# A fused linear-attention and gated-MLP block on one Trainium2 core: output weights from sixteen 32-column products, wider GELU pieces, and new engine orders

## The chip, the cores and the metric

The kernel runs on one core of one Trainium2 chip. The metric is the device time of one execution in microseconds (us); the number quoted for a kernel is the median of its runs.

The engines are named as in the profile: PE is TensorE's matmul stream, PEld its weight loads, DVE is VectorE, ACT is ScalarE, POOL is GpSimd and SP is the queue that issues most of the DMAs. A line number such as L547 is a line of the kernel before.

## The reference

Two blocks over one input `x` of 2048 tokens by 448 features (bfloat16):

```
h  = x + attention(layernorm(x))      # 16 heads of 28, phi(t) = (t > 0 ? t + 1 : exp(t)) + 1e-6
     kv  = sum over tokens of phi(k) v^T      (per head)
     z   = sum over tokens of phi(k)          (per head)
     o   = phi(q) kv / (phi(q) . z + 1e-6)
     attention = concat(o) @ wo
out = h + mlp(layernorm(h))           # gelu(h @ w_gate) * (h @ w_up) @ w_down, 1792 wide
```

There is no softmax, so the sum over all 2048 tokens has to be complete before any token gets its attention output. That gives the kernel two stages with a narrow passage between them.

## The kernel before, in words

Everything stays in the core's memories; the tokens are 16 tiles (0 to 15) of 128.

*First stage, up to about 33 us.* Each tile is normalised (`bnst1`, `bnag1`, `norm`), transposed (tiles 0 to 3 by PE, the rest by DMA, `xT`), and projected to keys (`k_t`, L469) and queries (`q_t`, L469). ACT takes exponentials of both (`ek`, `eq`) and the relu of the queries (`rq`); DVE turns the key part into phi(k) (`ck`, `pk`) and the query part into phi(q) (`cq` L564, `aq` L565). PE accumulates the "token product", the product of the normalised tokens and phi(k) over all tokens, in four PSUM banks (`pt`, L488). The value projection is applied afterwards to that product, so no value tensor is ever made.

*The passage, about 33 to 50 us.* The four banks of the token product are copied to SBUF: `evpD_3` (DVE, L516), `evpA_0` and `evpA_1` (ACT, L519), `evpD_2` (DVE, L521); `z1` (ACT, L514) and `z0` (DVE, L515) make the row sums z. `kv` (PE, L527, 16 small matmuls) multiplies by the value weights, `kvm` (DVE, L531) masks the result to the diagonal blocks of the heads, and `w2_0` to `w2_3` (PE, L547) multiply that by `wo`. The result, called the output weights here (`w2`), is a 448x448 matrix in four row chunks of 128; the last chunk has 64 rows, and they are there twice, because `kvd` (DVE, L536) duplicates the 64 columns of the stationary operand. `evw_0` to `evw_3` (L551, L553) copy the chunks to SBUF. Two DMAs on the SP queue (`dws0`, `dws1`) write the same weights with the two halves of the partitions exchanged into `w2s`, three chunks each.

At the same time the queries are divided by their denominators: `t1` (phi(q) times z, DVE for tile 0, POOL for the others, L569 and L585), `dr` (sum per head, DVE, L572 and L586), `deA`/`deP` (ACT adds 1e-6, L574 and L588), `rd` (reciprocal, DVE, L575 and L589), `pn` (multiplication, L576 and L590). The result is transposed (`tro` and `evo` for tiles 0 and 1, L599 and L602; a DMA `oT` for a later pair of tiles) and multiplied by `w2`: `out1_0` and `out1_1` (L617, 128 rows) for tiles 0 and 1, and for each later pair p of tiles (2p and 2p+1) `outA_p` and `outB_p` (L627, L628), whose matmuls use 64 rows, so that one of the upper and one of the lower half of the partitions go together. `hr` (DVE, L633) adds the residual, and the second layernorm follows (`bnst2`, `bnag2`, `ln2`, `rstd2` or POOL's `vpe2`, `pow2`, `negm2`; `nhD` or `nhP`). Tiles 0 and 1 are transposed by PE (`trh`, L654) and copied by ACT (`evh_0`, L658) and DVE (`evh_1`, L660); the others go by DMA (`hT`).

*Second stage, from about 50 us.* `gu_v` multiplies by gate and up weights (L731, L733; 64 rows, upper half gate, lower half up). The first four tiles go in chunks of two tiles (`gu2_0` to `gu2_13`, two column blocks of 128 for 256 tokens), the rest in chunks of four (`gu4_14` to `gu4_55`, one column block for 512 tokens). Each `gu` fills one gate bank and one up bank, and the banks alternate between two, so `gu_v+2` overwrites what `gu_v` wrote: it must wait for the GELU of `gu_v` (`ge`, ACT, L751) and for the multiplication that follows (`hm`, DVE, L753). Both are done in two halves of 256 columns, `ge0`, `ge1`, `hm0`, `hm1`. `down` (L697 in pairs of tiles, L678 for tiles 14 and 15) multiplies by the down weights, `fo` (L707, L682) adds the residual, and `do` (L708, L683) writes the tile to memory. Tile 15 is done in two column halves of 224, so that the first is written while the second is computed.

*What sets the order.* Nothing is reordered at run time: `ORDERS` (L15 ff.) holds one list of task numbers for each engine, and every engine works its list from first to last, waiting on semaphores. A task's number is its place in the program; the lists are the same tasks in another order. `HOLD` says for a task with several waits which of them comes first among them; the others are ordered by their counter. Each matmul that needs the task before it, and each buffer that is reused, is a wait in that list.

The tasks of PE in the passage stand in this order before the change: `pt3_15 q_5 q_4 kv q_7 q_8 w2_2 w2_0 w2_1 q_9 w2_3 tro_1 tro_0 q_6 out1_1 out1_0 q_10 q_11 q_13 q_12 q_14 q_15 trh_1 trh_0 outA_1 outB_1 gu2_0 gu2_1 outA_2 gu2_2 gu2_3 outB_2`. On DVE: `evpD_3 z0 aq_1 t1_0 dr_0 evpD_2 rd_0 dr_1 dr_2 kvm rd_2 kvd dr_3 rd_1 pn_0 rd_3 pn_1 evw_1 cqP_2 evw_3 pn_2 pn_3 aqP_2 hr_1 hr_0 bnst2_1 bnst2_0 bnag2_1 bnag2_0 drP_2 nhD_1 nhD_0 rdP_2 wr64_1 wr64_0 pnP_2 cqP_3 aqP_3 evh_1`.

Of the kernel before, what the change touches and what calls it, by code (L numbers as in the profile page):

```python
# [6 lines left out]
F32 = mybir.dt.float32  # L7
# [41 lines left out]
)  # L49
HOLD = {  # L50
    66: (36,), 141: (140,), 165: (164,), 214: (213,), 216: (215,), 323: (302,), 326: (324,), 431: (340,), 704:
    (564,), 735: (734,), 781: (672,), 839: (836,), 849: (846,), 854: (852,), 866: (865,),
}

# [768 lines left out]
```

## Time and profile before

| | |
|---|---|
| median of 3 runs | 190.59 us (190.46 to 190.67) |
| span of the profiled execution, first to last instruction | 188.3 us |
| what lies around the span, taken from that median | 2.3 us |
| mean granted TensorE clock | 1.000 |
| PE busy | 184.3 us, 1813 matmuls |
| DVE busy | 129.3 us, 330 instructions |
| ACT busy | 76.5 us, 220 instructions |
| POOL busy | 50.0 us, 91 instructions |

The profiled execution has no device time of its own in the records, only its span; the 2.3 us are the difference between the median and that span. A row of the timeline reads: start, duration, engine, line, operation, output and inputs, shape, number of instructions merged into the row, and in brackets the idle time before and who ended it. The duration of a matmul in such a row contains its way through the array, so consecutive matmuls overlap: what one costs in a sequence is read from the distance of the starts. A row of the chain of waits reads: start, the time that it has on the chain, and what ran.

### The profile page before, as it was taken

How to read it: one execution, taken by the hardware profiler on the slowest of the kernel's cores; microseconds unless marked ns; L12 is line 12 of the kernel's file. 1: busy time of each engine (PE TensorE's matmuls, PEld its weight loads, DVE VectorE, ACT ScalarE, POOL GpSimd, SP SyncE). 2: the span in 40 equal slices, each digit the busy share in tenths (PEclk: the TensorE clock that was granted, in tenths of full speed). 3: DMA queues.
4: the chain of work that ended last, by engine and by line, in shares of the span. 5: the costliest groups of instructions: out<-in, count | busy, mean ns of one | idle time of the engine just before them, and what ended most of it. 6: DMA issues, size and time to landing. Idle time of an engine off the chain costs nothing.

```text
span 188.3 us, 4459 instructions
## 1 busy us (share of the span) xinstructions
PE 184.3 (98%) x1813; PEld 109.2 (58%) x1813; DVE 129.3 (69%) x330; ACT 76.5 (41%) x220; POOL 50.0 (27%) x91
## 2 busy tenths in 40 slices
PE   7999999999999999999999999999999999999994
PEld 7545555555688788965554555555545545454554
DVE  4999959999899998786796762562645244335432
ACT  3878752799963231432234222321242222224100
POOL 6067910704505686033614000206100000000000
PEclk9999999999999999999999999999999999999999
DMA  5996458999393526820005720000096000002024
GB/s 169 387 231 88 96 104 194 218 222 174 65 320 64 95 52 116 84 52 0 0 3 98 144 54 0 0 3 2 3 135 111 3 0 24 3 0 98 3 79 140
DMA packets 35076, 17.11 MB, mean 91 GB/s; under 512 B 26864, under 2 KB 33648, under 8 KB 35056
## 3 DMA queue, kind: packets, MB, share of 16 engines
q1 hardware_dynamic: 34432, 16.32, 41.1%
q10 hardware_dynamic: 624, 0.52, 0.8%
q8 instruction: 14, 0.23, 0.5%
q14 instruction: 6, 0.05, 0.1%
HBM read 8.26 MB, written 1.84 MB: 54 GB/s over the span
## 4 chain that ended last, share of the span: by engine, by line
PE 94%; DVE 3%; DMA 1%; issue 0%
PE ps L733 38%; PE ps L697 19%; PE ps L469 12%; PE ps L731 9%; PE ps L488 6%; PE ps L627 3%; PE ps L678 3%; PE ps L628 2%; DMA x_sb<-in_A_x_dram 1%; DVE st L413 1%; PE ps L617 1%; PE ps L547 1%; PE ps L527 1%; PE ps L443 0%; PE ps L654 0%; DVE den L572 0%
## 5 line engine op out<-in xcount | busy, mean ns | idle before, releaser
L733 PE MATMUL ps<-hnT,wgu_sb 64*128 64x512 bf16 (+1 forms) x490 | 88.8, 333 | 0.0
L731 PE MATMUL ps<-hnT,wgu_sb 64*128 64x512 bf16 (+1 forms) x490 | 88.6, 333 | 0.0
L751 ACT ACTIVATE gl<-ps 128x256 bf16<-128x256 f32 x112 | 36.6, 383 | 85.3 <-PE ps L731 84.4
L753 DVE TENSOR_TENSOR hh<-ps,gl 128x256 bf16<-128x256 f32 x112 | 42.1, 416 | 41.4 <-ACT gl L751 41.3
L733 PEld LDWEIGHTS ps<-hnT,wgu_sb 64*128 64x128 bf16 x490 | 45.2, 94 | 32.9 <-DVE hh L753 3.4
L731 PEld LDWEIGHTS ps<-hnT,wgu_sb 64*128 64x128 bf16 x490 | 45.4, 94 | 2.5
L697 PE MATMUL ps<-wd_sb,hh 64*128 64x448 bf16 x392 | 41.5, 349 | 0.0
L697 PEld LDWEIGHTS ps<-wd_sb,hh 64*128 64x128 bf16 x392 | 23.2, 94 | 14.5
L469 PE MATMUL ps<-wqk_sb,xnT 128*128 128x448 bf16 x128 | 27.4, 353 | 0.0
L413 DVE BATCH_NORM_STATS2 st<-x_sb 128x6 f32<-128x448 bf16 x32 | 19.2, 612 | 1.8 <-DMA x_sb<-in_A_x_dram 1.7
L585 POOL TENSOR_TENSOR t<-pq,zbc 128x448 f32<-128x448 bf16 x12 | 12.3, 1042 | 23.7 <-DVE pq L583 22.0
L469 PEld LDWEIGHTS ps<-wqk_sb,xnT 128*128 128x128 bf16 x128 | 11.9, 98 | 11.4 <-DVE pk L482 0.8
L488 PE MATMUL ps<-pk,xnn 128*128 128x448 bf16 x64 | 13.9, 352 | 0.0
L627 PE MATMUL ps<-w,pqnT 64*128 64x448 bf16 x49 | 11.5, 349 | 0.1
L425 POOL TENSOR_SCALAR ln<-mv 128x2 f32<-128x2 f32 x7 | 2.0, 291 | 35.2 <-DVE mv L414 35.0
L480 ACT ACTIVATE e<-ps 128x448 bf16<-128x448 f32 x16 | 8.5, 539 | 5.6 <-PE ps L469 5.5
L628 PE MATMUL ps<-pt_sb,pqnT 64*128 64x448 bf16 x42 | 10.2, 350 | 0.0
L633 DVE TENSOR_TENSOR x_sb<-ps,x_sb 128x448 bf16<-128x448 f32 x16 | 9.6, 616 | 0.7 <-PE ps L628 0.6
L662 POOL TENSOR_SCALAR hn<-x_sb,nm,rs 128x448 bf16<-128x448 bf16 x14 | 9.9, 719 | 0.4
L482 DVE SCALAR_TENSOR_TENSOR pk<-ps,e 128x448 bf16<-128x448 f32 x16 | 9.8, 617 | 0.1
L488 PEld LDWEIGHTS ps<-pk,xnn 128*128 128x128 bf16 x64 | 6.3, 98 | 5.9 <-DVE pk L482 0.3
L453 POOL TENSOR_SCALAR xnn<-x_sb,nm,rs 128x448 bf16<-128x448 bf16 x12 | 8.9, 744 | 2.2 <-ACT rs L422 1.9
(85 smaller groups left out, 160.5 us busy)
## 6 DMA issues: line engine op xcount, KB each, us to landing
out_dram<-x_sb SPq DMA_DIRECT2D x15, 112.0 KB, 1.8
wd_sb<-in_B_w_down_dram SPq DMA_DIRECT2D x1, 1568.0 KB, 8.4
x_sb<-in_A_x_dram SPq DMA_DIRECT2D x3, 448.0 KB, 5.9
wgu_sb<-in_B_w_gate_dram SPq DMA_DIRECT2D x1, 896.0 KB, 12.1
wgu_sb<-in_B_w_up_dram SPq DMA_DIRECT2D x1, 896.0 KB, 16.5
wgu_sb<-in_B_w_gate_dram SPq DMA_DIRECT2D x1, 672.0 KB, 6.1
wgu_sb<-in_B_w_up_dram SPq DMA_DIRECT2D x1, 672.0 KB, 8.5
wo_sb<-in_A_wo_dram SPq DMA_DIRECT2D x1, 392.0 KB, 7.5
```

What stands on the lines that cost most here:

```text
L413: op("dve", lambda e: e.bn_stats(st[:, t, :], src_ap), [b_src], [b_st[t]], "bnst%s_%d" % (tag, t))
L469: ins = e.matmul(ps[:, bk, 0:D], xnT[:, t, k, :], wqk_sb[:, k, c0:c0 + D], start=(k == 0), stop=(k == 3))
L488: ins = e.matmul(ps[:, BK_PT[c], 0:D], xnn[:, t % XN_R, c * 128:(c + 1) * 128], pk[:, ip, :], start=(t == 0), stop=(t == T - 1))
L585: op("pool", lambda e, n=n: e.tensor_tensor(t1[:, n, :], pq[:, a + n, :], zbc[:, :], ALU.mult), [b_pq[a + n]] + b_z, [b_t1[n]], "t1p_%d" % ...
L627: e.matmul(ps[:, BK_OUT[0], 0:D], pqnT[ra, i2, sg // 2, :], w2[ra, sg // 2, :], start=(sg == 0), stop=(sg == 5))
L628: ins = e.matmul(ps[:, BK_OUT[1], 0:D], pqnT[rb, i2, 3 + (sg + 1) // 2, :], (w2 if sg == 6 else w2s)[rb, sg // 2, :], start=(sg == 0), sto ...
L662: op("pool", lambda e, t=t, sh=sh: e.tensor_scalar(hn[:, sh, 0:D], x_sb[:, t, :], nm2[:, t:t + 1], rs2[:, t:t + 1], ALU.add, ALU.mult), [b ...
L697: ins = e.matmul(ps[:, bko[half][n], 0:D], hh[rows, j, sl[n]], wd_sb[rows, j, :], start=(j == 0 and (half == 0 or p == 6)), stop=(j == NJ ...
L731: first = e.matmul(psG[:, jj * N:(jj + 1) * N], wgu_sb[A_, k, j * 128:(j + 1) * 128], hnT[A_, ka_, c0:c0 + N], start=(k == 0), stop=(k == ...
L733: ins = e.matmul(psU[:, jj * N:(jj + 1) * N], wgu_sb[B_, k, j * 128:(j + 1) * 128], hnT[B_, kb_, c0:c0 + N], start=(k == 0), stop=(k == NK ...
L751: G.add("act", lambda e, gi=gi, cs_=cs_, psG=psG: e.activation(gl[:, gi, cs_], psG[:, cs_], AF.Gelu_apprx_tanh), r=[b_ps[BK_G[i]]], w=[b_g ...
L753: op("dve", lambda e, dst=dst, srcU=srcU, srcL=srcL: e.tensor_tensor(dst, srcU, srcL, ALU.mult), [b_ps[BK_U[i]], b_glh], [b_ar[j_][t % HR] ...
```

## The change

It has six parts.

1. **Output weights.** `w2` is made by sixteen matmuls with 32 stationary columns each, in place of seven with 128. Each writes 32 of the 128 PSUM rows of a chunk. `kvd` is gone; the last chunk has its 64 rows once, the other 64 are zeroed at the start (`w2pad`, a DVE memset). The tail's copy for the other half of the partitions now comes with the transfer `dws1`, which moves four chunks in place of three.
2. **Token product.** The copy of bank 2 moves from DVE (`evpD_2`) to ACT (`evpA_2`).
3. **Denominator.** `t1` gets a 29th column per head that holds 1e-6, written once at the start; the sum per head is over 29 columns, and the ten ACT additions `deA` and `deP` are gone.
4. **GELU pieces.** For the chunks of two tiles (`gu2_0` to `gu2_13`), `ge` and `hm` are one instruction of 512 columns each in place of two of 256.
5. **Last tile.** Tile 15's columns are split 320 and 128 in place of 224 and 224.
6. **Orders.** All lists but SP's are written anew, and `HOLD` has 583 entries in place of 15. PE in the passage: `pt3_15 q_4 q_5 q_7 kv q_9 q_6 w2_1 w2_3 w2_2 w2_0 q_8 tro_0 tro_1 q_11 out1_0 out1_1 q_10 q_12 q_15 q_14 q_13 trh_0 trh_1 outA_1 outB_1 gu2_0 gu2_1 gu2_2 outA_2 gu2_3 gu2_4 outB_2`. DVE: `evpD_3 z0 t1_0 dr_0 rd_0 dr_1 rd_1 pn_1 pn_0 kvm dr_2 dr_3 rd_2 evw_1 rd_3 pn_2 evw_3 cqP_2 pn_3 cqP_3 aqP_2 cqP_4 hr_0 hr_1 bnst2_0 bnst2_1 bnag2_0 bnag2_1 drP_2 nhD_0 rdP_2 wr64_0 nhD_1 wr64_1 aqP_3 pnP_2 evh_1 hr_3 hr_2 bnst2_3 aqP_4 hm0_0 drP_3 hm0_1`; `cq_1`, `aq_1`, `aq_3` and others of that kind now stand among `ck_7` to `pk_14` of the first stage. ACT: `z1 evpA_1 evpA_0 rq_4 evpA_2 eq_5 rq_5 eq_4 rq_7 eq_7 eq_9 eq_6 evw_2 evw_0 rq_6 evo_0 evo_1 eq_8 rq_8 rq_9 rq_11 eq_11 eq_10 rq_10 rq_12 ln2_0 ln2_1 rstd2_0 eq_15 rstd2_1 rq_15 eq_14 rq_14 evh_0 eq_12 eq_13 rq_13 tbl2 ge0_0`. POOL's list differs in details (`powwarm` early, the two `t1p` of a pair exchanged). On PE, `outA_5`, `outB_5`, `outA_6`, `outB_6` stand earlier in the second stage, `downA_0` stands ahead of `outB_3`, and `downA_1`, `downB_1`, `downA_2` later.

The diff without the lists:

```diff
-        t1 = sb("t1", [128, 2, D], F32)
+        t1 = sb("t1", [128, 2, H, DH + 1], F32)
-        eps_d = sb("eps_d", [128, 1], F32)
+        t1f = t1[:].rearrange("p n h d -> p n (h d)")[:, :, 0:D]
-        w2s = pt_sb[:, 0:3, :]
+        w2s = pt_sb
+        op("dve", lambda e: e.memset(w2[B_, 3, :], 0.0), [], [b_w2t], "w2pad")
-        op("pool", lambda e: e.memset(eps_d[:], EPS), [], [b_epsd], "epsd")
+        op("pool", lambda e: e.memset(t1[:, :, :, DH:DH + 1], EPS), [], [b_epsd], "epsd")
...
-            if c in (0, 1):
+            if c in (0, 1, 2):
                 op("act", lambda e, c=c: e.activation(pt_sb[:, c, :], ps[:, BK_PT[c], 0:D], AF.Identity), ...
...
-        op("dve", lambda e: e.tensor_copy(kvz[:, 4 * D:4 * D + 64], kvz[:, 4 * D - 64:4 * D]), [b_kvm], [b_kvd], "kvd")
-        def kvc(g, c):
+        def kvc(g, c, q):
             o = g * D + c * 128 if c < 3 else 4 * D - 64
-            return kvz[:, o:o + 128]
+            return kvz[:, o + 32 * q:o + 32 * q + 32]
-        for c in range(4):
+        for c, parts in enumerate((((0, 0), (1, 0), (2, 0), (3, 0), (3, 1)), ((0, 1), (1, 1), (2, 1), (3, 2)),
+                                   ((0, 2), (1, 2), (2, 2), (3, 3), (2, 3)), ((0, 3), (1, 3)))):
...
-                for g in gs:
-                    ins = e.matmul(ps[:, BK_W2[c], 0:D], kvc(g, c), wo_sb[:, g, :], start=(g == gs[0]), stop=(g == gs[-1]))
+                for i, (q, g) in enumerate(parts):
+                    ins = e.matmul(ps[32 * q:32 * q + 32, BK_W2[c], 0:D], kvc(g, c, q), wo_sb[:, g, :],
+                                   start=q not in [x[0] for x in parts[:i]], stop=q not in [x[0] for x in parts[i + 1:]])
...
-            dma("sp", w2s[to, :, :], w2[of, 0:3, :], [b_w2s[h]], "dws%d" % h, r=b_w2[0:3], after=xts[-1:])
+            dma("sp", w2s[to, 0:3 + h, :], w2[of, 0:3 + h, :], [b_w2s[h]], "dws%d" % h, r=b_w2[0:3 + h], after=xts[-1:])
...
-                    op("act", lambda e, i=i: e.activation(den[:, i, :], den[:, i, :], AF.Identity, bias=eps_d[:, 0:1]), ..., "deA_%d" % t)
-                op("act", lambda e: e.activation(den[:, i:i + 2, :], den[:, i:i + 2, :], AF.Identity, bias=eps_d[:, 0:1]), ..., "deP_%d" % p)
...
-            parts = [...] if t < T - 1 else [(BK_L[t][0], 0, D // 2), (BK_L[t][1], D // 2, D)]
+            parts = [...] if t < T - 1 else [(BK_L[t][0], 0, 320), (BK_L[t][1], 320, D)]
...
-                for hh_ in range(2):
-                    cs_ = slice(hh_ * 256, (hh_ + 1) * 256)
+                for hh_ in range(2 if nj == 1 else 1):
+                    cs_ = slice(hh_ * 256, (hh_ + 1) * 256) if nj == 1 else slice(0, 512)
```

In `parts` of a chunk, the first number of a pair is the quarter of 32 columns (and of 32 PSUM rows), the second the group of four heads. `t1_3` also gets a wait for `pn_0`.

More of the change, by code (lines that the diff above doesn't have):

```diff
@@ L523, in fkv @@
-        def fkv(e):
-            ins = None
-            for g in range(NG):
-                for c in range(4):
-                    ins = e.matmul(ps[0:GW, BK_KV, g * GW:(g + 1) * GW], wv_sb[:, c, g * GW:(g + 1) * GW], pt_sb[:, c, g * GW:(g + 1) * GW],
-                                   start=(c == 0), stop=(c == 3))
-            return ins
-        G.add("pe", fkv, r=b_wv + [b_wpad[1]] + b_pt, w=[b_ps[BK_KV]], name="kv")
-        op("dve", lambda e: e.tensor_tensor(kvz[:, 0:5 * D].rearrange("p (g c) -> p g c", g=NG)[:, :, 0:GW].rearrange("p g (h f) -> p g h f", h=4),
-                                            ps[0:GW, BK_KV, 0:D].rearrange("p (g h f) -> p g h f", g=NG, h=4),
-                                            mask[:, :].unsqueeze(1).unsqueeze(3).to_broadcast([GW, NG, 4, DH]), ALU.mult),
-           [b_ps[BK_KV], b_mask, b_kvm], [b_kvm], "kvm")
@@ new lines, in fkv @@
+        def fkv(e):
+            ins = None
+            for g in range(NG):
+                for c in range(4):
+                    ins = e.matmul(ps[0:GW, BK_KV, g * GW:(g + 1) * GW], wv_sb[:, c, g * GW:(g + 1) * GW], pt_sb[:, c, g * GW:(g + 1) * GW],
+                                   start=(c == 0), stop=(c == 3))
+            return ins
+        G.add("pe", fkv, r=b_wv + [b_wpad[1]] + b_pt, w=[b_ps[BK_KV]], name="kv")
+        op("dve", lambda e: e.tensor_tensor(kvz[:, 0:5 * D].rearrange("p (g c) -> p g c", g=NG)[:, :, 0:GW].rearrange("p g (h f) -> p g h f", h=4),
+                                            ps[0:GW, BK_KV, 0:D].rearrange("p (g h f) -> p g h f", g=NG, h=4),
+                                            mask[:, :].unsqueeze(1).unsqueeze(3).to_broadcast([GW, NG, 4, DH]), ALU.mult),
+           [b_ps[BK_KV], b_mask, b_kvm], [b_kvm], "kvm")
@@ L611, in a2_pair @@
+        for h, (to, of) in enumerate(((A_, B_), (B_, A_))):
+            dma("sp", w2s[to, 0:3 + h, :], w2[of, 0:3 + h, :], [b_w2s[h]], "dws%d" % h, r=b_w2[0:3 + h], after=xts[-1:])
+        def a2_pair(p):
+            a = 2 * p
+            i2 = p % 2
+            if True:
+                a2_den(p)
             if p == 0:
@@ L669, in b2_tile @@
         def b2_tile(t):
[L670 removed]
+            parts = [(BK_L[t][0], 0, D)] if t < T - 1 else [(BK_L[t][0], 0, 320), (BK_L[t][1], 320, D)]
             for bk, c0, c1 in parts:
```

78 lines of the change are left out of this document (36 added, 42 removed), and 139 rows, old and new, of tables (HOLD, ORDERS).

## The prediction, made before the changed kernel ran

> **What bounds the kernel now.** I read the page first: busy times, the slices, the shares of the chain that ended last.
>
> ```profile
> span 188.3 us, 4459 instructions
> PE 184.3 (98%) x1813; PEld 109.2 (58%) x1813; DVE 129.3 (69%) x330; ACT 76.5 (41%) x220; POOL 50.0 (27%) x91
> ...
> DVE  4999959999899998786796762562645244335432
> ...
> PE 94%; DVE 3%; DMA 1%; issue 0%
> ```
>
> PE has work nearly all the time, so a faster DVE or ACT instruction gains nothing by itself. Time can go only where PE waits, where its own work shrinks, or after its last matmul. In slices 2 to 16 (to about 75 us) DVE is at nine tenths, so a wait for DVE is what PE risks there. The chain in order of time shows the one place where PE visibly waits in the middle:
>
> ```profile
> 35.38 0.54 DVE pt_sb L521
> ...
> 35.96 1.03 PE ps L527 x16
> ...
> 38.51 1.14 PE ps L547 x6
> ...
> 40.40 0.19 PE ps L547
> ...
> 47.85 0.78 PE ps L654 x14
> ```
>
> DVE's copy of bank 2 (L521) is the last thing that `kv` waits for. Six `w2` matmuls take 1.14 us on the chain: 0.19 us for each matmul of 448 columns. The timeline of PE gives the starts:
>
> ```profile
> 34.23 1.68 PE L469 MATMUL ps<-wqk_sb,xnT 128*128 128x448 bf16 x8
> 35.96 1.03 PE L527 MATMUL ps<-pt_sb,wv_sb 128*112 128x112 bf16 x16
> 36.83 1.68 PE L469 MATMUL ps<-wqk_sb,xnT 128*128 128x448 bf16 x8
> ...
> 47.69 0.94 PE L654 MATMUL ps<-ident,hn 128*128 128x128 bf16 x14
> 48.57 0.36 PE L627 MATMUL ps<-w,pqnT 64*128 64x448 bf16 x1
> 48.57 0.36 PE L628 MATMUL ps<-pt_sb,pqnT 64*128 64x448 bf16 x1
> ...
> 50.14 0.27 PE L733 MATMUL ps<-hnT,wgu_sb 64*128 64x256 bf16 x1
> ```
>
> Eight projections from 34.23 would end at 34.23 + 8 x 0.19 = 35.74; `kv` starts at 35.96: PE lost 0.22 us. The fourteen transposes end at 47.69 + 0.78 = 48.47 and the first 64-row matmul starts at 48.57: 0.10 us go where the shape of the tiles changes. The two rows at 48.57 start together, so matmuls on different parts of the array do run side by side.
>
> **Part by part.** All sums are against the span of 188.3 us; the median of the runs, 190.59, lies 2.3 us above it, and I carry these 2.3 over.
>
> *Token product on ACT, and the order before `kv`.* ACT's rows for this and a later step:
>
> ```profile
> 34.43 0.98 ACT L519 ACTIVATE pt_sb<-ps 128x448 bf16<-128x448 f32 x2 [1.16 <-PE ps L488]
> ...
> 51.12 1.28 ACT L762 ACT_TABLE_LOAD   x1
> 52.41 0.66 ACT L751 ACTIVATE gl<-ps 128x256 bf16<-128x256 f32 x2
> ```
>
> ACT's two copies of 0.54 take 0.98 together, so starts on ACT follow each other by 0.44 us. Next in its list stand `rq_4` (35.31) and `evpA_2`, which so runs from 35.75 to 36.30. PE now has `q_7` too ahead of `kv`: 35.74 + 0.76 = 36.49. The wait is covered by 0.2 us and gone: -0.22. If ACT came 0.2 us later the wait would be back.
>
> *Sixteen products.* Before: 1.14 + 0.19 = 1.33 us. Each new matmul still streams 448 columns, 0.19 us, but four column quarters can run side by side. Starts follow the program in every PE row, so I count rounds in the written order (`w2_1 w2_3 w2_2 w2_0`): quarters 0,1,2,3 / 0,1 / 0,1,2,3 / 2,0,1 / 2,3 / 3. That is six rounds, 1.13 us, and the tile shape changes twice, 0.20 us at the price of 48.57: 1.33, no gain. The ends: four rounds with no price for the change, 0.76, which is -0.57; all sixteen in turn, 3.02 + 0.20, which is +1.89. I take six rounds, since the row-halves at 48.57 show overlap but nothing here shows a matmul passing a blocked one. The Trainium skill (TensorEngine Tiling (Array Packing), Key Properties) states that changing the tiling mode drains the engine; the 0.10 us at 48.57 agrees.
>
> `kvd` (0.14 us of DVE) goes too, hidden already. The larger `dws1` has an issue at about 41.7; the two transfers landed 5.7 us after issue, so 47.4 or, with four chunks for three, at most 49.3; `outA_1`, which waits for it, is due at 48.4. I take 47.5 and no wait, since 5.7 us is mostly not size:
>
> ```profile
> pt_sb<-w SPq DMA_DIRECT2D x2, 168.0 KB, 5.7
> ```
>
> *From `out1` to the first `gu`.* `kv` 36.49 + 0.87, two projections tiles 1.51, `w2` 1.33, `q_8` 0.76, eight transposes 0.45, `q_11` 0.76: `out1_0` starts at 42.16, `out1_1` at 42.91, five query tiles follow to 47.44, where `trh_0` is due (47.69 before). DVE's part in between:
>
> ```profile
> 42.77 1.20 DVE L633 TENSOR_TENSOR x_sb<-ps,x_sb 128x448 bf16<-128x448 f32 x2
> ...
> 47.06 0.20 DVE L647 COPY hn<-hn 128x64 bf16<-128x64 bf16 x2
> 47.18 1.09 DVE L590 TENSOR_TENSOR pqn<-pq,rd 128x896 bf16<-128x896 bf16 x1
> ...
> 48.60 0.63 DVE L583 TENSOR_TENSOR pq<-pq,eq 128x896 bf16<-128x896 bf16 x1
> 49.15 0.62 DVE L660 COPY hnT<-ps 128x896 bf16<-128x896 bf16 x1
> ```
>
> From `hr` to the end of the second `wr64` it took 47.26 - 42.77 = 4.49 us. Now `hr_0` waits for `out1_0` (four matmuls, 42.16 + 3 x 0.19 + 0.35 = 43.1) and `hr_1` a further 0.2 for `out1_1`: `wr64_1` ends at 47.85, `trh_1` is due at 47.83 and waits 0.07 with the hop. `outA_1` starts near 48.4 (48.57 before), `outB_1` ends near 49.95. `evh_1` stands behind `aqP_3` and `pnP_2`, 0.63 + 1.09 less their overlaps, and ends at 49.97: `gu2_0` at 50.02, 0.12 earlier than before.
>
> *Wide GELU and a third `gu` in a row.* `gu2_2` now has only `gu2_1` between itself and `gu2_0`. A `gu2` takes 1.52 us of PE, so it is due at 50.02 + 3.05 = 53.07, and must wait for the whole multiplication of `gu2_0`. The starts of `gu2_1` and `gu2_2` before:
>
> ```profile
> 51.67 0.27 PE L733 MATMUL ps<-hnT,wgu_sb 64*128 64x256 bf16 x1
> ...
> 53.95 0.27 PE L733 MATMUL ps<-hnT,wgu_sb 64*128 64x256 bf16 x1
> ```
>
> and in the groups by line and shape (count | busy us, mean ns):
>
> ```profile
> L753 DVE TENSOR_TENSOR hh<-ps,gl 128x256 bf16<-128x256 f32 x112 | 42.1, 416 | 41.4 <-ACT gl L751 41.3
> L751 ACT ACTIVATE gl<-ps 128x256 bf16<-128x256 f32 x112 | 36.6, 383 | 85.3 <-PE ps L731 84.4 <-DVE mv L414 0.9
> L551 ACT ACTIVATE w<-ps 128x448 bf16<-128x448 f32 x2 | 1.0, 541 | 0.0
> L553 DVE CAST w<-ps 128x448 bf16<-128x448 f32 x2 | 1.2, 617 | 0.0
> ```
>
> From 256 and 448 columns, 512 columns are 0.60 us on ACT and 0.69 on DVE. ACT's list without the `deA` reaches `tbl2` about half a microsecond earlier (`eq_10` waits for `q_10` until 44.6, then come nine query pieces of 0.44, the small `ln2` and `rstd2`, and `evh_0`): table loaded at 51.85, GELU to 52.45, multiplication to 53.15, `gu2_2` at 53.20, 0.13 late. Before, it started at 53.95 behind `outA_2` (four rounds, 0.75), so at the same point of the work 53.20. Up to here the change is worth 0.00: what `kv` gave is used up in the new waits. The ends are -0.45, if `w2` takes four rounds and both chains move with it, and +0.7, if DVE comes to `hm0_0` one 0.6 us instruction late.
>
> Every later chunk of two tiles has an `out` or a `down` between itself and the `gu` whose banks it takes; `gu4_14`, which takes those of `gu2_12`, has none, now as before:
>
> ```profile
> 80.81 0.38 PE L731 MATMUL ps<-hnT,wgu_sb 64*128 64x512 bf16 x1
> 80.98 0.39 PE L733 MATMUL ps<-hnT,wgu_sb 64*128 64x512 bf16 x1
> ```
>
> There the second matmul came 0.17 us after the first, which it accompanies elsewhere: a wait for the multiplication. The wide pair needs 1.29 us and hops where the halves needed about as much: -0.05.
>
> *Denominator.* `deA` and `deP`, ten ACT pieces, stand on no step that PE waits for; the sums grow by 1/28 of their streaming time. Zero. The `cq` and `aq` that move into the first stage find DVE idle there, in front of the `ck` of L481:
>
> ```profile
> DVE e L481 <- ACT e L480: 2.2, 3, 1.0
> ```
>
> Six pieces of 0.3 to 0.4 us fit into these 2.2 us. Zero, and +0.3 at most if one `pk` comes late.
>
> *Last tile.*
>
> ```profile
> 180.43 5.45 PE ps L678 x42
> ```
>
> on the chain, and in the timeline
>
> ```profile
> 184.56 0.39 DVE L682 TENSOR_TENSOR x_sb<-ps,x_sb 128x224 bf16<-128x224 f32 x1 [0.72 <-PE ps L678]
> 184.98 1.67 SPq L683 DMA_DIRECT2D out_dram<-x_sb  x2
> 185.90 0.39 DVE L682 TENSOR_TENSOR x_sb<-ps,x_sb 128x224 bf16<-128x224 f32 x1 [0.95 <-PE ps L678]
> ```
>
> and, of the weight loads in the groups,
>
> ```profile
> L678 PEld LDWEIGHTS ps<-wd_sb,hh 128*128 128x128 bf16 x42 | 4.0, 98 | 1.6 <-issue 0.4
> ```
>
> The number of columns is the same, 320 + 128, and fourteen transposes of 128 columns with their weight loads took 0.78 us (0.056 each), so PE ends when it did. The last DVE piece shrinks from 0.39 to about 0.29 (0.62 for 448 columns, L553): -0.10. The write of the 320 columns, though, is now issued only half a microsecond ahead of the last one instead of 1.3; if the queue holds the last one up, +0.1 to +0.2. I take -0.05.
>
> Sum: 0.00 - 0.05 - 0.05 = -0.10; 188.2 us of span, 190.5 us of device time.
>
> **The rivals.** *Four rounds (faster).* If the 32-column products overlap beyond the written order, PE, and behind it ACT and DVE, come 0.35 to 0.45 earlier to `gu2_0` and `gu2_2`: with the -0.10, 190.0 to 190.15. For: side-by-side starts at 48.57. Against: two quarters are asked for twice in a row.
>
> *In turn (slower).* If the column quarters share one stream, +1.89: 192.4. Against it again the rows at 48.57, which are row halves, however.
>
> *DVE late for the wide pieces (slower).* `hr_3`, `hr_2`, `bnst2_3` and `aqP_4` stand ahead of `hm0_0`, and `drP_3` (about 1.1 us) ahead of `hm0_1`; the wide multiplication can't start on a half. If DVE is 0.4 us or more behind my count at 52.45, `gu2_2` and then `downA_0` (due near 63.0, its last-but-one `hm` at 62.85) wait: +0.35 to +0.7, 190.9 to 191.2. For: DVE's nines. Against: it loses `evpD_2`, `kvd` and `aq_1` ahead of that.
>
> *Narrow last matmuls (slower).* The Trainium skill (TensorE: Matmul & The Clock Gate, Back-to-back issue gap) gives about 81 ns a matmul at 128 columns in a stream with weight loads. By that the last fourteen would take 1.13 us, not 0.78. As a mechanism of this kernel: the weight load, 98 ns a piece in the rows of L678, becomes the bound below 224 columns, 14 x 0.098 = 1.37 in place of 0.78, at most +0.6, 191.1; it decides if loads don't overlap one another. The transposes at 47.69, with a load each, speak against it.
>
> **How the numbers follow.** A measurement of this kernel tells about 0.2% (0.38 us) from no change. Forecast (about equal, 190.2 to 190.95): 0.42. Four rounds, or waits smaller than I counted: 0.34. DVE late: 0.14; narrow last matmuls: 0.04; in turn: 0.06. So faster 0.34, same 0.42, slower 0.24. The range takes the forecast, four rounds with the full 0.57 and the tail's 0.15 (189.8), and DVE late up to 191.1.
>
> **What would show it.** Right: no idle time before L527; six distinct starts in the sixteen `w2` matmuls and 0.1 us before and after them; `gu2_0` near 50.0, `gu2_2` near 53.2 with a wait for DVE's multiplication in front; the last DVE piece 0.29 us. Wrong: four starts and `gu2_2` before 52.9; or `w2` over 3 us; or PE idle in front of `downA_0` or several `gu2`; or a spacing above 0.056 us in the last fourteen matmuls.

## The result, and the profile after

The changed kernel takes 189.65 us (median of 6 runs, 189.58 to 189.77) against 190.63 us of the kernel before beside it (190.46 to 191.13): a ratio of 0.9942, 95% interval 0.9928 to 0.9957. That is 0.98 us less, well beyond what can be told from no change, and just below the forecast range, whose lower end the prediction works out as 189.8. The page of the changed kernel:

```profile
span 187.7 us, 4436 instructions
PE 183.3 (98%) x1822; PEld 123.4 (66%) x1822; DVE 129.1 (69%) x315; ACT 73.7 (39%) x197; POOL 52.6 (28%) x91
...
PE 96%; DVE 2%; DMA 1%; issue 0%
```

The span is 0.6 us shorter than the 188.3 of before, and PE carries 96% of the chain in place of 94%. Line numbers are shifted in the changed kernel, and again in each experiment, because the written-out lists differ in length: `kv` is L651 here, the output weights L668, `q` L542, `trh` L729. PE's timeline, against the one shown in the prediction:

```profile
34.31 2.43 PE L542 MATMUL ps<-wqk_sb,xnT 128*128 128x448 bf16 x12
36.58 0.99 PE L651 MATMUL ps<-pt_sb,wv_sb 128*112 128x112 bf16 x16
37.41 1.68 PE L542 MATMUL ps<-wqk_sb,xnT 128*128 128x448 bf16 x8
39.01 0.94 PE L668 MATMUL ps<-wo_sb,hh 112*32 112x448 bf16 x16
39.88 0.93 PE L542 MATMUL ps<-wqk_sb,xnT 128*128 128x448 bf16 x4
...
43.37 3.95 PE L542 MATMUL ps<-wqk_sb,xnT 128*128 128x448 bf16 x20
47.19 1.08 PE L729 MATMUL ps<-ident,hn 128*128 128x128 bf16 x14
48.20 0.36 PE L702 MATMUL ps<-w,pqnT 64*128 64x448 bf16 x1
...
49.77 0.28 PE L808 MATMUL ps<-hnT,wgu_sb 64*128 64x256 bf16 x1
...
52.83 0.27 PE L806 MATMUL ps<-hnT,wgu_sb 64*128 64x256 bf16 x1
52.88 0.28 PE L808 MATMUL ps<-hnT,wgu_sb 64*128 64x256 bf16 x1
```

Read by the distance of the starts:

- Twelve projections take 12 x 0.189 = 2.27 us: 34.31 + 2.27 = 36.58, exactly where `kv` starts. The wait of 0.22 us is gone.
- The output weights hold PE from 39.01 (eight projections from 37.41 would end at 38.92, so 0.09 us go at the change of tile shape) to 39.88: 0.87 us, with the 0.09 in front 0.96, where the prediction counted 1.33.
- Twenty projections from 43.37 end at 47.15; the fourteen transposes begin at 47.19 and then need 1.01 us to the first 64-row matmul at 48.20, where before they needed 0.88 (47.69 to 48.57). Here 0.04 and 0.11 us are new waits, for VectorE's normalised tiles.
- The second row of `gu2_2` starts 0.05 us behind the first (52.83, 52.88): a short wait for the multiplication of `gu2_0`.

So PE is 0.37 us earlier at `outA_1` (48.20 against 48.57) and at `gu2_0` (49.77 against 50.14), and stays there. How sixteen matmuls fit into 0.87 us is seen when the same view is asked for windows that end at 39.15, 39.35 and 39.55; the last number is how many have started:

```profile
39.01 0.37 PE L668 MATMUL ps<-wo_sb,hh 112*32 112x448 bf16 x4
...
39.01 0.56 PE L668 MATMUL ps<-wo_sb,hh 112*32 112x448 bf16 x8
...
39.01 0.75 PE L668 MATMUL ps<-wo_sb,hh 112*32 112x448 bf16 x12
```

Four rounds of four, 0.19 us apart, not six. The tail, in the rows of VectorE:

```profile
184.71 0.49 DVE L757 TENSOR_TENSOR x_sb<-ps,x_sb 128x320 bf16<-128x320 f32 x1 [1.28 <-PE ps L753]
185.49 0.29 DVE L757 TENSOR_TENSOR x_sb<-ps,x_sb 128x128 bf16<-128x128 f32 x1 [0.29 <-PE ps L753]
```

The last piece starts 0.41 us earlier than before (185.49 against 185.90), ends 0.51 us earlier, and the span, 0.6 us shorter, takes a last 0.07 from a quicker last write. PE's last fourteen matmuls, of 128 columns each, start 0.056 us apart, as the transposes do.

### The profile page after: what moved, and what is told of

Same layout as the page of the kernel before. It is cut to its first block, busy times and chain, and to the rows that moved or that the text cites. A ratio compares the mean times of both kernels' runs of the same rounds, so it can differ in the third digit from the quotient of the medians.

```text
span 187.7 us, 4436 instructions
## 1 busy us (share of the span) xinstructions
PE 183.3 (98%) x1822; PEld 123.4 (66%) x1822; DVE 129.1 (69%) x315; ACT 73.7 (39%) x197; POOL 52.6 (28%) x91
## 4 chain that ended last, share of the span: by engine, by line
PE 96%; DVE 2%; DMA 1%; issue 0%
PE ps L808 24%; PE ps L806 22%; PE ps L772 19%; PE ps L542 13%; PE ps L561 6%; PE ps L702 3%; PE ps L753 3%; PE ps L703 2%; DMA x_sb<-in_A_x_dram 1%; DVE st L486 1%; PE ps L692 1%; PE ps L729 1%; PE ps L668 0%; PE ps L516 0%; PE ps L651 0%; DVE xnn L508 0%
## 5 line engine op out<-in xcount | busy, mean ns | idle before, releaser
L826 ACT ACTIVATE gl<-ps 128x256 bf16<-128x256 f32 (+1 forms) x98 | 35.7, 415 | 88.1 <-PE ps L806 88.0
L828 DVE TENSOR_TENSOR hh<-ps,gl 128x256 bf16<-128x256 f32 (+1 forms) x98 | 41.0, 454 | 41.4 <-ACT gl L826 41.0
L808 PEld LDWEIGHTS ps<-hnT,wgu_sb 64*128 64x128 bf16 x490 | 45.4, 94 | 13.1 <-DVE hh L828 1.5
L772 PE MATMUL ps<-wd_sb,hh 64*128 64x448 bf16 x392 | 40.6, 349 | 0.0
L772 PEld LDWEIGHTS ps<-wd_sb,hh 64*128 64x128 bf16 x392 | 26.6, 94 | 11.0
L542 PE MATMUL ps<-wqk_sb,xnT 128*128 128x448 bf16 x128 | 27.4, 353 | 0.0
L542 PEld LDWEIGHTS ps<-wqk_sb,xnT 128*128 128x128 bf16 x128 | 12.0, 98 | 11.4 <-DVE pk L555 0.7
L613 POOL TENSOR_TENSOR t<-pq,zbc 128x448 f32<-128x448 bf16 x12 | 13.1, 1113 | 17.7 <-DVE pq L611 10.7
L703 PE MATMUL ps<-pt_sb,pqnT 64*128 64x448 bf16 x49 | 11.5, 349 | 0.0
L737 POOL TENSOR_SCALAR hn<-x_sb,nm,rs 128x448 bf16<-128x448 bf16 x14 | 10.1, 733 | 0.5
```

Source lines behind the costliest of these rows:

```text
L542: ins = e.matmul(ps[:, bk, 0:D], xnT[:, t, k, :], wqk_sb[:, k, c0:c0 + D], start=(k == 0), stop=(k == 3))
L613: op("pool", lambda e, n=n: e.tensor_tensor(t1[:, n, :, 0:DH], pq[:, a + n, :].rearrange("p (h d) -> p h d", h=H), zbc[:, :].rearrange("p ...
L703: ins = e.matmul(ps[:, BK_OUT[1], 0:D], pqnT[rb, i2, 3 + (sg + 1) // 2, :], w2s[rb, sg // 2, :], start=(sg == 0), stop=(sg == 5))
L737: op("pool", lambda e, t=t, sh=sh: e.tensor_scalar(hn[:, sh, 0:D], x_sb[:, t, :], nm2[:, t:t + 1], rs2[:, t:t + 1], ALU.add, ALU.mult), [b ...
L772: ins = e.matmul(ps[:, bko[half][n], 0:D], hh[rows, j, sl[n]], wd_sb[rows, j, :], start=(j == 0 and (half == 0 or p == 6)), stop=(j == NJ ...
L808: ins = e.matmul(psU[:, jj * N:(jj + 1) * N], wgu_sb[B_, k, j * 128:(j + 1) * 128], hnT[B_, kb_, c0:c0 + N], start=(k == 0), stop=(k == NK ...
```

## The experiments

Each kernel ran beside the kernel before on the same chip, five rounds except where said; ratios are against that. The experiments ran on several chips, so a ratio compares better across them than a time does. "Quickest" is the lowest single time.

**The control: how much lies around the span, and how steady are the two kernels?** The kernel before again, and the changed kernel again, nothing edited.

> The kernel before, unchanged, so that its spans are seen beside its times. The profiled execution of before had a span of 188.26 us, 2.37 below the median of 190.63; after has 187.68 and 189.66, 1.98 apart. If what lies around the span is 1.98 for both (theory A), the spans of before are near 188.65 and its profiled execution was 0.4 us quicker than usual, by a wait that comes and goes; then this run's profile may show it, PE waiting for a transposed tile in the first stage. If the surroundings differ (theory B), spans stay near 188.25 and the time around them at 2.35.

> The changed kernel, nothing edited, beside the kernel before on one chip. Theory A: its span is the 187.7 us of its trace in nearly every execution and 2.0 us lie around it, so 189.6 to 189.8 us, while the kernel before varies from 190.2 to 191.3. Rival: the narrow spread of its first six executions (189.58 to 189.77) was chance; then single executions come up to 1 us later here too, and the median near 190.0.

The kernel before: 190.68 us (190.29 to 191.33, ratio 1.0011, 0.9999 to 1.0023). Its spans go from 188.3 to 189.3, and time minus span is 2.0 us in every execution (190.32 with 188.3, 191.33 with 189.3). The changed kernel: 189.73 us (ratio 0.9948, 0.9929 to 0.9967), five of six executions from 189.56 to 189.83 and one at 190.36. So the 2.3 us that the prediction carried were 2.0, and the profiled execution of before was a quick one, about 190.3 us. Of the 0.98 us between the medians, 0.6 separate the two quick executions; the rest, 0.3 to 0.4, is that a typical execution of the kernel before lies 0.3 to 0.6 above its quickest one, and of the changed kernel only 0.1 to 0.2.

The profiles tell where this lies. Cut each span at two starts of PE: that of the projections ahead of `kv` (34.23 before, 34.31 after) and that of `gu2_0`. Between them, in what is called the passage below, the kernel before takes 15.91 to 15.92 us in five profiles (before, e1, e10, f1, g1) and the changed kernel 15.46 to 15.50 in six (after, e5, e6, e7, e11, f5). From `gu2_0` to the end it is 138.11 to 138.13 and 137.90 to 137.91 us (e7 apart, which undoes the last tile). So the change is worth 0.45 us in the passage and 0.2 behind it, and what differs between executions of one kernel lies ahead of the passage. With these two stretches an edit is judged to a few hundredths of a us, where a median of twelve is good to about 0.2.

**The sixteen products.** Alone in the kernel before (with the exchange tail; `w2_3` ahead of `q_9`); undone in the changed kernel; and issued quarter by quarter (three rounds):

```diff
 e2: before, PE  - w2_2 w2_0 w2_1 q_9 w2_3      + w2_2 w2_0 w2_1 w2_3 q_9   (the 16 matmuls of the change)
 e3: after       - 16 matmuls of 32 columns     + 7 of 128 columns, kvd, transfers of 3 chunks
 e4: after       - for c, parts ...: for (q, g) in parts: matmul(...)
                 + for q in range(4): for c in (1, 3, 2, 0): for g in groups of (c, q): matmul(...)
```

> Before with the sixteen products and the exchange transfer of the tail alone (the second output-weight group now in one piece ahead of the next query tile). Theory A: four rounds make the passage 0.3 to 0.4 us shorter for PE, but DVE's chain behind it (evw, pn, hr) is unchanged, so 0.0 to 0.35 comes through: ratio 0.998 to 1.000. Theory B (orders and the hold table made the gain): ratio 1.000. Serial products would give 1.008.

> After with seven products of 128 columns, the duplicated 64 columns and three-chunk transfers put back, all orders as in after. Theory A: 0.3 to 0.45 us of the gain is lost, 189.95 to 190.1, ratio 0.9965 to 0.998. Theory B: 189.65, ratio 0.995.

> After with the sixteen products issued quarter by quarter, all four of a quarter in a row, in place of turn by turn. If each quarter has its own deep queue, still four rounds of 0.19 us and a time within 0.2 us of after. If matmuls start strictly as written, 13 rounds at the least, 2.4 us, and 1.5 to 1.8 us more: 191.2 to 191.5. A short window gives something between.

Alone: 190.39 us, ratio 0.9999 (0.9986 to 1.0012), no gain that can be told; the passage is 15.80 us, 0.11 shorter. Undone: 190.13 us, ratio 0.9978 (0.9966 to 0.9989), 0.4 to 0.5 more than the changed kernel in time and 0.6 by the ratios; the passage is 15.84 us, 0.38 longer than the 15.46 of the changed kernel. In the profile of the first, PE has the 0.87 us, and then `tro` starts late:

```profile
38.70 0.94 PE L530 MATMUL ps<-wo_sb,hh 112*32 112x448 bf16 x16
39.58 0.93 PE L456 MATMUL ps<-wqk_sb,xnT 128*128 128x448 bf16 x4
40.58 0.62 PE L584 MATMUL ps<-ident,pqn 128*128 128x128 bf16 x8
```

Four projections from 39.58 end at 40.34; the transposes come at 40.58, 0.24 us late, behind ScalarE's copy of an output chunk whose bank they take. Quarter by quarter, the starts are still four rounds of four:

```profile
39.85 0.40 PE L1156 MATMUL ps<-wo_sb,hh 112*32 112x448 bf16 x4
...
39.85 0.59 PE L1156 MATMUL ps<-wo_sb,hh 112*32 112x448 bf16 x8
...
39.85 0.78 PE L1156 MATMUL ps<-wo_sb,hh 112*32 112x448 bf16 x12
```

The first four in that program all go to quarter 0, the next four to quarter 1, and so on. If each had to start in the written order, quarter after quarter would take its turn and there would be thirteen rounds, 2.5 us. There are four, so a matmul for a free quarter passes one that waits for a busy quarter. The Trainium skill (TensorE: Matmul & The Clock Gate, Part 3, The mechanism) states that matmuls are strictly first in, first out in their starts and ends, without reordering; by that the thirteen rounds would be due, and these runs show otherwise for the starts of tiles of 32 columns.

The signals are another matter, and the time was not within the expected 0.2 us: 191.07 us (ratio 1.0020, 1.0000 to 1.0039), the quickest 190.2, 0.6 above the changed kernel's quickest. The passage takes 16.08 us in place of 15.46. VectorE's copy of the first chunk waits for the signal of the thirteenth matmul, the first one of quarter 3, which as a member of the first round would be done at 40.25 (39.85 + 0.40); the copy starts at 40.89, 1.04 us after the first of the sixteen, when the last of them ends, in place of 0.43 us in the changed kernel (the second row):

```profile
40.89 0.62 DVE L1163 CAST w<-ps 128x448 bf16<-128x448 f32 x1 [0.56 <-PE ps L1156]
```
```profile
39.44 0.62 DVE L676 CAST w<-ps 128x448 bf16<-128x448 f32 x1
```

So matmuls pass each other in their starts, but here the result was not announced any earlier for it; PE then waits 0.05 us at the transposes, 0.13 at `out1` and 0.42 at `trh`. That some executions take 191.0 to 191.6 and others 190.2 to 190.3 has another cause, below.

**Bank 2 on ScalarE, and both PE parts together.** The copy and `q_7` ahead of `kv` alone, in two orders; then with the sixteen products:

```diff
 e8: before, ACT - z1 evpA_0 evpA_1 deA_0    + z1 evpA_0 evpA_1 evpA_2 deA_0     (DVE: evpD_2 removed)
     PE          - kv q_7 q_8 w2_2 w2_0 w2_1 q_9 w2_3 tro_1 tro_0 q_6 out1_1 out1_0 q_10
                 + q_7 kv q_8 q_9 w2_2 w2_0 w2_1 q_6 w2_3 tro_1 tro_0 q_10 out1_1 out1_0
 f3: as e8, PE   - tro_0 q_10 out1_1 out1_0 q_11     + tro_0 q_11 out1_1 out1_0 q_10
 f4: as f3 with the 16 matmuls, PE - w2_1 q_6 w2_3   + w2_1 w2_3 q_6
```

> The kernel before, with the copy of bank 2 on ScalarE and q_7 ahead of kv (q_8 and q_9 then stand between kv and w2, q_6 between w2_1 and w2_3, q_10 ahead of out1_1); nothing else of the change. Theory A: the 0.22 us of wait in front of kv go, 190.3 us against 190.5. Rival: a wait in front of the transposes or of out1 takes their place, since ScalarE has 0.44 us more to do ahead of them: 190.5 to 190.7.

> The kernel before with the copy of bank 2 on ScalarE and q_7 ahead of kv once more, now with q_11 in place of q_10 ahead of out1_1, so that no query tile waits for a bank that ScalarE still reads (1.99 us in the first version). Theory A: the wait in front of kv goes and nothing takes its place: 0.2 us under the kernel before beside it, 190.3. Rival: ScalarE, with 0.44 us more to do, makes the transposes or out1 wait: 190.5 or more.

> The kernel before with the two parts that shorten TensorE's own work and waits, bank 2 on ScalarE and sixteen products, in an order of TensorE as in the last kernel; deA, halves of GELU and the rest as before. Theory A: both gains of the trace add up, 0.22 + 0.37: 190.0 against 190.5. Rival: the gains are not to be had without the orders and without the end of deA, since ScalarE and VectorE reach the transposes, trh and the first gu no earlier: 190.3 to 190.6.

The first gave 193.13 us (1.0117, 1.0096 to 1.0137), for a reason of my own making: `q_10` takes the bank of `q_6`, whose exponential stands behind the copies of the transposes in ScalarE's list.

```profile
41.38 0.61 PE L584 MATMUL ps<-ident,pqn 128*128 128x128 bf16 x8
43.81 0.93 PE L454 MATMUL ps<-wqk_sb,xnT 128*128 128x448 bf16 x4 [1.83 <-ACT eq L481]
```

Without that wait: 190.81 us, ratio 1.0009 (1.0000 to 1.0019), no gain, and a passage of 16.16 us in place of 15.91; with the sixteen products as well: 190.72 us, ratio 1.0008 (0.9997 to 1.0019), still none, 16.01 us. The timeline of the last shows both gains made and lost:

```profile
35.66 1.11 PE L456 MATMUL ps<-wqk_sb,xnT 128*128 128x448 bf16 x5
36.61 0.99 PE L514 MATMUL ps<-pt_sb,wv_sb 128*112 128x112 bf16 x16
37.50 1.69 PE L456 MATMUL ps<-wqk_sb,xnT 128*128 128x448 bf16 x8
39.12 0.94 PE L530 MATMUL ps<-wo_sb,hh 112*32 112x448 bf16 x16
39.99 0.93 PE L456 MATMUL ps<-wqk_sb,xnT 128*128 128x448 bf16 x4
40.95 0.62 PE L584 MATMUL ps<-ident,pqn 128*128 128x128 bf16 x8
...
43.68 4.27 PE L456 MATMUL ps<-wqk_sb,xnT 128*128 128x448 bf16 x20
47.79 0.94 PE L639 MATMUL ps<-ident,hn 128*128 128x128 bf16 x14
48.67 0.36 PE L612 MATMUL ps<-w,pqnT 64*128 64x448 bf16 x1
...
50.35 0.27 PE L716 MATMUL ps<-hnT,wgu_sb 64*128 64x256 bf16 x1
```

`kv` follows its five last projections without a gap (35.66 + 5 x 0.189), and the output weights cost 0.96. But `q_8` starts 0.07 us late, the transposes wait 0.20 us, and the twenty projections take 4.11 us up to `trh` in place of 3.78; all of this waits for ScalarE, for its reads of their banks and its copy of an output chunk. `gu2_0` comes 0.11 us later than the last `outB_1` would let it. Some 0.6 us gained, 0.7 lost before `gu2_0`.

**The orders alone.** The computations of the kernel before in the lists of the changed one (`evpD_2` behind `dr_0`, `kvd` behind `kvm`, `deA_t` and `deP_p` put into ScalarE's list).

> The computations of the kernel before (seven products, bank 2 on VectorE, deA and deP on ScalarE, halves of GELU, 224 and 224) in the orders of the changed kernel. Theory A: the orders alone take the wait in front of kv away and nothing else, 190.3 us, with the spread of the kernel before. Rival: the orders are what makes the executions alike and the second stage earlier: 189.9 to 190.1 and a spread below 0.4 us. Third: with deA and deP in ScalarE's list, VectorE waits for it in the passage, 190.6 or more.

193.82 us (1.0157, 1.0135 to 1.0179). The new lists put `rd` close behind `dr`, and with `deA` between them VectorE and ScalarE wait for each other in turn:

```profile
41.26 0.31 ACT L1126 ACTIVATE den<-den,eps_d 128x16 f32<-128x16 f32 x1 [1.66 <-DVE den L1124]
...
42.23 0.25 DVE L1127 RECIPROCAL rd<-den 128x16 f32<-128x16 f32 x1 [1.00 <-ACT den L1126]
...
43.02 0.93 PE L1151 MATMUL ps<-ident,pqn 128*128 128x128 bf16 x8 [0.74 <-DVE w L1105]
```

Neither these two parts without the lists nor the lists without the parts give a gain that can be told. My places for `deA` and `deP` are part of this loss, so it says that the end of these steps is needed for such lists, not what it is worth.

**The smaller parts, undone one at a time in the changed kernel.**

```diff
 e6: - for hh_ in range(2 if nj == 1 else 1)   + for hh_ in range(2)        (halves of GELU and product)
 e7: - (0, 320), (320, D)                      + (0, D // 2), (D // 2, D)   (last tile 224 and 224)
 e11: - 583 entries of HOLD                    + the 15 of the kernel before
 e10 (in the kernel before): - 15 entries      + the 583, as far as the tasks exist
```

> The changed kernel with GELU and the multiplication of the chunks of two tiles in halves of 256 columns again. Theory A: the wide pair needs 1.32 us from its start to its end in the trace of the changed kernel (ge0_0 at 51.50, hm0_0 to 52.82), two halves there and in the other chunks about 1.17 us, so the wait of 0.045 us in front of gu2_2 may go and nothing else changes: the same as the changed kernel beside it within 0.1 us, 189.7. Rival: the fourteen more instructions on each engine make VectorE late in its full stage: 0.2 to 0.5 us more, 189.9 to 190.2.

> The changed kernel with tile 15 split 224 and 224 again. Theory A: PE ends when it did, the last DVE piece takes 0.39 us again and the last write lands a little later: 0.10 to 0.17 us more than the changed kernel beside it, 189.75 to 189.85. Rival: the split brings nothing, because the write of the 320 columns holds the last one up: no difference.

> The changed kernel with the fifteen HOLD entries of the kernel before. Theory A: no difference, 189.7 with most executions between 189.5 and 189.9. Rival: without the 583 entries the executions spread over 1 us again and the median is 190.0 or later.

> The kernel before, its orders unchanged, with the order of the waits of one instruction (HOLD) taken from the changed kernel as far as the same tasks exist. Theory A: which of several waits is held first makes no time: 190.5 to 190.7, and single executions from 190.2 to 191.3. Rival: the 583 entries are what makes the executions alike: 190.0 to 190.3 with a spread below 0.5 us.

Halves: 189.73 us, ratio 0.9960 (0.9945 to 0.9975), no difference: passage and rest are 15.46 and 137.90 us as in the changed kernel. The multiplication of `gu2_0` then starts at 52.05 as it does wide at 52.13, behind `aqP_4` on VectorE both times. Last tile: 189.89 us, 0.16 more than the control beside it (189.73). The ratio, 0.9963 (0.9950 to 0.9976), overlaps that of the control, but the stretch behind `gu2_0` is 138.07 us in place of 137.90, 0.17 more. HOLD: 189.80 us (0.9966, 0.9951 to 0.9982) without the 583 entries, 190.64 with them in the kernel before (1.0004, 0.9991 to 1.0018): nothing either way.

**An attempt at better: the new waits of `trh` taken away.**

```diff
 e12: after, DVE - nhD_0 rdP_2 wr64_0 nhD_1 wr64_1 aqP_3 pnP_2 evh_1
                 + nhD_0 wr64_0 nhD_1 wr64_1 rdP_2 aqP_3 evh_1 pnP_2
```

> The changed kernel with VectorE's order in the passage nhD_0 wr64_0 nhD_1 wr64_1 rdP_2 aqP_3 evh_1 pnP_2, so that trh_0 and trh_1 no longer wait 0.04 and 0.11 us. Theory A: the gain is lost again at gu2_2, since ScalarE's last query pieces and the loading of its table (50.15 to 51.43 us) set when ge0_0 can start: the wait of 0.045 us there becomes about 0.2, and the time stays at 189.7. Rival: gu2_2 comes earlier too, 189.55.

190.11 us, ratio 0.9980 (0.9966 to 0.9993), by the medians 0.3 to 0.4 slower than e6 and e11 beside it, by the quickest 0.25; both expectations miss. The passage is 0.07 us shorter (15.39) and the stretch behind it 0.29 longer (138.20). The waits at `trh` shrink to 0.08 us, but VectorE, now with `evh_1` in front of `pnP_2`, is later everywhere behind it (`pnP_2` itself takes 1.60 us in place of 1.08), and `gu2_2` waits for the multiplication:

```profile
48.15 0.62 DVE L1217 COPY hnT<-ps 128x896 bf16<-128x896 bf16 x1
48.69 1.60 DVE L1099 TENSOR_TENSOR pqn<-pq,rd 128x896 bf16<-128x896 bf16 x1
...
52.34 0.68 DVE L1310 TENSOR_TENSOR hh<-ps,gl 128x512 bf16<-128x512 f32 x1
...
52.68 0.27 PE L1288 MATMUL ps<-hnT,wgu_sb 64*128 64x256 bf16 x1
53.07 0.28 PE L1290 MATMUL ps<-hnT,wgu_sb 64*128 64x256 bf16 x1
```

The step that sets `gu2_2` is VectorE's full list from `pnP_2` to `hm0_0`, not the loading of ScalarE's table, which was 0.08 us earlier here (50.07).

**Why the kernel before is less steady.** What differs between executions lies ahead of the passage. Part of it is the first loads of `x`: in eleven of the twenty profiles, of either kernel, PE waits 0.09 to 0.42 us at 10.1 to 10.8 us, and in nine of these VectorE is seen waiting 0.11 to 0.37 us for a piece of `x` at 8.2 to 8.8, as in none of the other nine profiles. Then there are loads of instructions (queues q8 and q14 of the DMA view). In all twenty profiles every transposing transfer that takes over 0.3 us longer than the quickest of its place has such a load in its time. That the load is what lengthens it is read from this coincidence, and not each load does: of two transfers under way it is mostly the older that takes longer, and some loads lengthen none (e7's at 18.71). Two kinds matter. First, `xT_4`, which `k_4` needs at 14.6: it lands 3.2 to 3.5 us after its issue in sixteen profiles, where the 16 KB load starts at 14.7 to 15.8, and 4.7 to 4.9 us after it in four (e4, e7, e9, g2), where the load starts at 13.1 to 13.6. In e7, its transfer, its load (packets, MB, share of the DMA engines between 13.4 and 14.7 us; the changed kernel has none in that window), and `k_4`:

```profile
DMA to landing us min/median/max: 4.9/4.9/4.9
```
```profile
q8 instruction: 1, 0.02, 4.7%
```
```profile
15.57 0.92 PE L1024 MATMUL ps<-wqk_sb,xnT 128*128 128x448 bf16 x4 [0.58 <-DMA xnT<-xnn]
```

That execution took 190.76 us, the slowest of its twelve; the profiled executions of e9 and g2 were the slowest of theirs too, and that of e4 (191.11) belongs to its late group. Second, an 8 KB load at 25.3 to 27.2 us. With the kernel before and its orders (before, e1, e2, e8, e10, f1, f3, f4) the older transfer at that time is `xT_13`, which then takes 3.2 to 3.6 us in place of 2.5; in the other twelve it is `xT_14` (3.0 to 3.3). In the kernel before `xT_13` is due at once: it lands at 26.58, `k_13` starts at 26.66. In the changed kernel `xT_14` lands at 27.68, `k_14` starts at 28.26. The tile view of the transfers `xT_12` and `xT_13` of the kernel before (the longest is `xT_13`'s):

```profile
L455 SPq DMA_TRANSPOSE xnT<-xnn x2: 1264/1264/1264, 22.0 to 23.3; - x2
...
DMA to landing us min/median/max: 2.5/2.9/3.2
```

In e10, where it came later, PE waited:

```profile
27.55 0.92 PE L1021 MATMUL ps<-wqk_sb,xnT 128*128 128x448 bf16 x4 [0.47 <-DMA xnT<-xnn]
```

Four runs tried this: `k_13` made later in the kernel before, `k_14` made earlier in the changed kernel, and the lists up to the last token product exchanged both ways.

```diff
 f1: before, PE - k_13 pt4_9    + pt4_9 k_13
 f5: after, PE  - pt4_9 k_14    + k_14 pt4_9
 g1: before, lists of PE, ACT, DVE, POOL up to pt3_15, z1, evpD_3, t1_1: - its own  + those of after (without aq_1)
 g2: after, the same                                                     - its own  + those of before, then aq_1
```

> The kernel before with k_13 and pt4_9 exchanged on TensorE, so that k_13 is due 0.76 us later. Theory C: in the kernel before the transposing transfer xT_13 takes 3.2 to 3.5 us in place of 2.5, because a load of instructions falls into it at 25.3 to 26.3 us, and lands 0.1 us ahead of k_13 or up to 0.6 us late; with the later k_13 the executions come together at the quick end: median 190.3 and most of them within 0.3 us. Rival: the spread comes from the first loads of x and of the weights (before 9 us), as in one execution of the changed kernel; then median and spread stay, 190.5 to 190.6, 190.2 to 191.3.

> The changed kernel with k_14 ahead of pt4_9, due 0.76 us earlier, at 27.5. Theory C: there the load of instructions falls into xT_14, which lands at 27.7 to 28.4, 0.6 us ahead of k_14 as it stands; with the earlier k_14 TensorE waits 0.2 to 0.8 us in front of it and the median is 189.9 to 190.3 with a spread like that of the kernel before. Rival: no difference, 189.7, since a wait there is caught up or the transfers are quick in most executions.

> The kernel before with the orders that the changed kernel has up to the last token product (TensorE, ScalarE, VectorE without the later aq_1, GpSimd); all behind it as before. Theory D: the first-stage orders are what brings the executions together, since a load of instructions no longer falls into a transfer that is due at once: quickest 190.2, median 190.25 to 190.35. Rival: the distance of the median from the quickest is none of theirs: median 190.5 to 190.65 as in the kernel before beside it.

> The changed kernel with the orders that the kernel before has up to the last token product (aq_1 at their end, powwarm ahead of negm2_2). Theory D: quickest 189.6, median 189.9 to 190.1. Rival: median 189.65 to 189.75 as in the changed kernel.

f5 did as the theory says: 190.08 us (0.9974, 0.9962 to 0.9986), 0.35 above the changed kernel, with PE waiting 0.32 us for `xT_14`:

```profile
26.30 1.68 PE L1024 MATMUL ps<-wqk_sb,xnT 128*128 128x448 bf16 x8
28.13 0.92 PE L1024 MATMUL ps<-wqk_sb,xnT 128*128 128x448 bf16 x4 [0.15 <-DMA xnT<-xnn]
```

f1 tells nothing: 190.78 us (1.0009, 0.9998 to 1.0019), with a new wait of 0.32 us for VectorE's `pk` at 30.2 that covers whatever was freed. g1: 190.47 us against 190.71 beside it, in the direction and of the size of the theory, but its ratio, 0.9991 (0.9977 to 1.0005), takes in no change. g2: 190.17 us (0.9969, 0.9958 to 0.9980), 0.44 above the control of the changed kernel; its quickest is 0.37 later as well, though, so that is not steadiness alone. Three of the query pieces (`aq_3`, `cq_1`, `aq_1`) there stand last in VectorE's list, hold up `evpD_3`, and leave `trh_0` a wait of 0.22 us in place of 0.04; the passage is 0.18 us longer (15.64).

```profile
33.37 0.39 DVE L1076 TENSOR_TENSOR pq<-pq,eq 128x448 bf16<-128x448 bf16 x1
33.68 0.61 DVE L1122 CAST pt_sb<-ps 64x448 bf16<-64x448 f32 x1
```

## Why the prediction was wrong

The forecast was 190.5 us; it is 189.65. The step that failed is "Sixteen products", where it says "I take six rounds": 0.00 was put down for a part that is worth 0.37 us on PE (1.33 to 0.96), and 0.38 us of the passage when it alone is undone (e3). Its end of -0.57 had the four rounds right and left out the shape changes, which do cost 0.09 and 0.10. The argument against four rounds was "starts follow the program in every PE row"; all those rows were of tiles that cover the whole array or alternate its two halves, so they could not show it. Point by point:

- *Token product on ACT*: right, -0.22, `kv` at 36.58 against 36.49 forecast, no wait. f3 adds that the same edit in the old surroundings gives nothing: ScalarE's later query pieces cost more than the 0.22.
- *"Up to here the change is worth 0.00"*: the mechanism was right, some gain is used up in new waits. The sizes were not: 0.15 us at `trh` and none that count later, against 0.59 gained. With 0.08 us of later first loads in this execution (the first `k` starts at 6.40 against 6.32) that makes the -0.37 at `gu2_0`. There it was forecast at 50.02, `gu2_2` at 53.20 with 0.13 of wait; they came at 49.77 and 52.83 with 0.05.
- *`gu4_14`, -0.05*: the wait of 0.145 us went, and gained nothing, since only one of the two row halves was late: all of the matmuls behind it are 0.37 us earlier, as those ahead. A gap in one row of two is not a gap of PE.
- *Denominator, zero*: no price was found for it alone, but "stand on no step that PE waits for" held for the old lists only. e9 shows what `deA` does in the new ones, and f3 and f4 show ScalarE as what eats the other gains while `deA` is there. That its end is what makes room is argued from these, not shown by a run that undoes it alone.
- *Early `cq` and `aq`, zero*: g2 shows up to 0.18 us at `trh_0` if they stay late. VectorE had idle time for them there, as said, but the gain behind it was not counted.
- *Last tile, -0.05*: -0.17 in the trace, +0.16 when undone. The fear that the write of the 320 columns holds up the last one (0.1 to 0.2 us) did not come true.
- *The 2.3 us around the span*: 2.0 in every execution. The profiled execution of before was a quick one; the prediction's own time for it was 0.3 too high, and nothing in it asked how far a typical execution lies above the profiled one. A third of the result is there. That this third comes from the first stage is seen in where executions differ; that the 8 KB load ahead of `k_13` is its main cause is argued from e10 and f5, which show what such a load can do, and not settled: f1 made a wait of its own, and the interval of g1 takes in no change.

Of the rivals, *Four rounds* (0.34) named the main cause; its 190.0 to 190.15 were 0.35 to 0.5 us too high, for the tail and the last point. *In turn* and *Narrow last matmuls* fell: sixteen matmuls took 0.87 us, and the last fourteen of the tail are 0.056 us apart, not the 0.081 that the prediction cites nor the 0.098 of a weight load; the tail starts 0.42 us earlier (179.94 against 180.36), and the last VectorE piece 0.41. *DVE late for the wide pieces* is half there: VectorE does set `gu2_2`, at a price of 0.05 us, and e12 shows what the rival meant when VectorE is held back further: a wait of 0.39 us in one row, 0.29 us on the stretch behind `gu2_0`.

## What to carry to other kernels

Small matmuls that use a quarter of the array's columns each can be counted as four independent queues: for PE's own time the longest queue counted here, not the written order. The order still counted for who got a result first (e4). Where two engines are as full as ScalarE and VectorE are here, a gain on a third shows only if their lists get room for it; test the parts together as well as alone. And before a difference of 0.5% is forecast from one profile, ask where that execution lies among the kernel's own; cutting the span at a few landmarks shows which stretch varies and which does not.

## What the runs showed of the hardware that was not expected

- Four column quarters ran four matmuls at a time, 0.19 us a round at 448 columns, whether the program went chunk by chunk or quarter by quarter. Written quarter by quarter, the signal of the thirteenth released its reader only 1.04 us after the first start, when all sixteen had run.
- A change of tile shape cost 0.09 to 0.10 us each time, from 128 to 32 columns and back as at the 64-row matmuls. The Trainium skill (TensorEngine Tiling (Array Packing), Key Properties) says that the mode change drains the engine; the trace agrees and gives the price.
- A transposing transfer into which a load of instructions fell took 0.7 us longer with one of 8 KB (`xT_13`, 2.5 to 3.2 us; 3.6 in e10) and 1.5 us with one of 16 KB (`xT_4`, 3.3 to 4.8), though not every load did this; what it cost depended on how soon the tile was due: nothing with 0.6 us to spare, 0.3 to 0.7 us where it came too late (f5, e10, e7). The Trainium skill (Runtime: NRT & Kernel Launch, Instruction fetch mechanics) calls the cost of fetching the next block of instructions mostly hidden; that held here except where the transfer beside it was itself on the path.
